# Loading the first w_in piece behind v, seven more magnitudes as VectorE masks, and other steps for the early pieces

## The chip, the cores and the metric

The kernel runs on one core of a Trainium2 chip. The metric is the device time of one execution in microseconds (us); the time given for a kernel is the median of its runs. Engines are named as in the profile: PE is TensorE, DVE is VectorE, ACT is ScalarE, POOL is GpSimd, and SP is the engine whose queue issues nearly all DMAs.

## The reference

Packed attention (32 packed queries per head, 8 batches, 8 heads, 576 tokens, 64 wide) feeds a feed-forward layer with a leaky activation:

```python
p_packed = sm_attn(p, k, v)                # 32 x 576 scores per head
out      = sm_attn(q, p_packed, p_packed)  # 576 x 32 scores per head
x = out as 4608 tokens x 512
h = x @ w_in                               # 512 x 2048
g = maximum(h, 0) + alpha * minimum(h, 0)
return g @ w_out                           # 2048 x 512
```

w_in and w_out are float64: the kernel turns them to float32 on the core, from their 32-bit words.

## The kernel before, in words

Work goes by batch b (0 to 7), each with two half-tiles of 288 tokens, k = 2b and 2b + 1. For a batch, `attention(b)` runs in small steps (it is a generator): load k, v, q; scores; softmax; `aT` (the transposed softmax) times v gives c, and its transposition p2 (p in the profile); scores against q; a second softmax over 32 entries; and the result a_f. The product h = x @ w_in is done as a @ (p2 @ w_in): `packed_w(b, j)` makes pw = p2 @ w_in for 512 columns (L375), `first(k, f)` makes 128 hidden rows (L774 in float32; L780 to L782 in split form), ACT takes the negative part (neg, L787), DVE adds the two parts to g (L801), and `second(k, f)` multiplies g by w_out into four accumulators (L896 in float32; L899 to L901 in split form). `first` writes to ps_h, a pool of two PSUM banks, so the third `first` needs the bank that the g of the one before last has set free.

w_in and w_out come in eight pieces of 1 MB each: `w_in_load`/`w_in_convert` and `w_out_load`/`w_out_convert`. A piece is converted in one of two forms. `to_f32` makes the magnitude of the upper word, then on DVE a clamp (L132), a shift (L135), the sign (L139) and the low word (L143), with ACT making the low word ready (L131). `to_half` has on DVE a clamp (L166), a shift (L169) and one addition (L177), and on ACT two instructions (L175, L176). The magnitude is one instruction in either: Abs on ACT (L151), or a mask on DVE (L123, only the first piece of w_in before).

The order is written out by hand. The string in `go` is the start: a and b are steps of attention(0) and attention(1), i and o load a piece of w_in or w_out, I and O convert one, 0 makes half of a packed product, H splits the float32 a of batch 0 in two, S splits the first pieces of w_out, n loads alpha, and u, v, w, x are spare matmuls that keep PE busy. After it come steps: step i issues `first` of the i-th (k, f) and `second` of the one two before, and `pieces` says which letters stand at which step. `PAIRS` are the steps with the packed products of both first batches. The program's scheduler then sets each engine's order; every engine works through its own order and waits at an instruction until what it needs is there. All loads go through SP's queue. An issue takes one of eight semaphores in turn and waits for the DMA that had it before.

Of the kernel before, what the change touches and what calls it, by code (L numbers as in the profile page):

```python
# [27 lines left out]
def pack_attention_ffn_kernel(  # L28
# [17 lines left out]
    nc = tc.nc  # L46
# [72 lines left out]
    def to_f32(raw, mag, on_dve=False):  # L119
        u, up, low = words(raw, "low", U32)  # L120
        bits = mag.bitcast(U32)
        if on_dve:
            nc.vector.tensor_scalar(  # L123
                out=bits, in0=u[:, :, :, 1], scalar1=0x7FFFFFFF, scalar2=None, op0=ALU.bitwise_and
            )
        else:
            magnitude(mag, up)
        with ExitStack() as behind:
            for mark in late + lows:
                behind.enter_context(tc.issue_after(mark.ins))  # L130
            lows[:] = [nc.scalar.activation(out=low, in_=u[:, :, :, 0], func=AF.Copy, scale=2.0**-29)]  # L131
        nc.vector.tensor_scalar(  # L132
            out=mag, in0=mag, scalar1=F64_BOTTOM, scalar2=F64_TOP, op0=ALU.max, op1=ALU.min
        )
        nc.vector.tensor_scalar(  # L135
            out=bits, in0=bits, scalar1=3, scalar2=0x3FFFFFF8,
            op0=ALU.logical_shift_left, op1=ALU.bitwise_and,
        )
# [8 lines left out]
    def magnitude(mag, up):  # L147
        with ExitStack() as behind:
            for ins in lows:
                behind.enter_context(tc.issue_after(ins.ins))  # L150
            nc.scalar.activation(out=mag, in_=up, func=AF.Abs)  # L151

    def to_half(raw, mag, begun=False):

        u, up, rest = words(raw, "rest", F32)
        bits = mag.bitcast(U32)
        low = rest.bitcast(U16).rearrange("p a (f t) -> p a f t", t=2)[:, :, :, 0]
        if not begun:
            magnitude(mag, up)
# [12 lines left out]
        if len(first_half) == 1:  # L178
            first_half.append(last)
# [10 lines left out]
        if written:  # L190
            queue[:] = [ins]

    first_half, begun = [], []
    last_mm, queue, written, raws, tail, whole, w0, other = [], [], [True], {}, {}, [], [], []

    def half(g):
        return g != 2

    def half_in(j):
        return j > 1  # L200

    def w_out_load(g):
        raws["o", g] = const.tile([P, 2, 512], U64, name=f"wraw{g}", tag=f"wo{g}")
# [2 lines left out]
    def w_out_convert(g):  # L206
        if g < QF:
            if not whole:
                whole.append(const.tile([P, QF, 2, 512], F32, name="wo_whole", tag="wo7"))
            mag = whole[0][:, g]  # L210
            for a in range(2):
                wo_t[2 * g + a] = mag[:, a]
        else:
            mag = cv.tile([P, 2, 512], F32, name="mag", tag="mag")
        if half(g):
            to_half(raws.pop(("o", g)), mag, g in begun)
        else:
            to_f32(raws.pop(("o", g)), mag)
        if g >= QF:
            w_out_split(g, mag)  # L220

    def w_out_begin(g):
        whole.append(const.tile([P, QF, 2, 512], F32, name="wo_whole", tag="wo7"))
        raw = raws["o", g]
        up = raw.bitcast(F32).rearrange("p a (f t) -> p a f t", t=2)[:, :, :, 1]
        nc.scalar.activation(out=whole[0][:, g], in_=up, func=AF.Abs)
        begun.append(g)
# [29 lines left out]
    def w_in_convert(n):  # L257
# [1 line left out]
        raw = raws.pop(("i", n))  # L259
        w = win.tile([P, 4, 256] if j == 0 else [P, 2, 512], F32, name="w", tag="w")  # L260
        if half_in(j):
            to_half(raw, w)
        else:
            to_f32(raw, w, n < 1)
        if j == 0:
            w0.append(w)
            for a in range(2):
# [680 lines left out]
    EARLY, XF, XJ, QF = 2, 1, 1, 2  # L948

    a0, a1 = attention(0), attention(1)  # L950
    counts = dict.fromkeys("iIoOSH01A", 0)
    BUSY = {"u": 7, "v": 4, "w": 2, "x": 3, "y": 3, "z": 2}
    BEHIND = {"v": "m0", "w": "z0", "z": "m1"}

    def go(what):


        for ch in what:
# [7 lines left out]
            elif ch in "ab":  # L966
                next(a0 if ch == "a" else a1, None)
            elif ch in counts:
                n = counts[ch]
                counts[ch] += 1  # L970
                if ch == "0":
                    if n < 2:
                        packed_w(0, 0, (n,))
                    else:
                        packed_w(0, n - 1)
                elif ch == "1":
                    packed_w(1, n, (None,) if n else (0, 1))
# [12 lines left out]
    go("inaaauoiaaaIaboaiiaa0abooavbawaOIx")  # L990
    tail.clear()
    written.clear()

# [10 lines left out]
            if b % 2 and k % 2:  # L1004
                order += [(b // 2, n, "columns") for n in range(4)]
    turns, joints, drains = {}, {}, []
    PAIRS = {13: ((1, 0), (1, 1)), 31: ((0, 2), (1, 2)), 35: ((0, 3), (1, 3))}
    for at_, pair in PAIRS.items():
        joints[at_] = [(0, packed_w_pair(*pair))]

# [7 lines left out]
                turns.setdefault(at_, []).append(gen)  # L1018
        drains.append((steps[-1], gen))

    pieces = {0: "aab", 1: "Oai0ib", 3: "bbI", 4: "I", 5: "Oob0", 6: "bbbiO", 7: "HHbb", 10: "S", 11: "S", 12: "b", 13: "bb", 14: "b", 15: "o", 17: "Io", 18: "b", 19: "I", 20: "i", 21: "o", 22: "I", 24: "I", 27: "O", 30: "O", 34: "O", 36: "O"}

    X = {1: 50, **{b: begins[b] + 8 for b in range(2, 7)}}
    Y = {1: 54, **{b: begins[b] + 22 for b in range(2, 7)}}
    for b in range(2, B):
        T, x, y = begins[b - 1], X[b - 1], Y[b - 1]
        if b == 2:
            firsts = [39, 40, 41, 42, 44, 45, 46, 47, 49]
        elif b == 3:
            firsts = [44, 50, 61, 62, 63, 64, 66, 67, 68]  # L1030
# [97 lines left out]
```

## Time and profile before

| | before |
|---|---|
| median of 3 runs | 711.91 us (711.72 to 712.71) |
| profiled execution | 712.62 us, of it span 710.8 us |
| PE busy | 695.5 us, 98% of the span |
| DVE busy | 474.3 us, 67% |
| ACT busy | 358.1 us, 50% |
| mean granted clock of PE | 0.995 of full |

The span is what the profiler saw from the first to the last instruction; the 1.8 us around it are in the time and not in the trace. PE is busy nearly all the time, so the end is set by when PE gets its work going at the start, and by each gap in it after that. The averages of DVE and ACT hide that both are full in the first stage.

### The profile page before, as it was taken

What the parts mean: (1) busy time and instruction counts of PE and PEld (TensorE: products, weight loads), DVE (VectorE), ACT (ScalarE), POOL (GpSimd) and SP (SyncE); (2) the same over time, 40 slices, a digit from 0 to 9 for tenths busy, and PEclk for the clock granted to TensorE, in tenths of its full rate; (3) what the DMA queues carried; (4) which work ended last, traced back from release to release, by engine and by line L of the source; (5) the groups of instructions that cost most, each with busy time, mean ns of one, the idle gap of its engine ahead of it and who ended that gap; (6) DMA issues with size and microseconds to landing.
All of it is one profiled execution on the core that took longest, in us unless ns stands there. A gap on an engine that the chain in (4) does not pass through costs nothing.

```text
span 710.8 us, 14597 instructions
## 1 busy us (share of the span) xinstructions
PE 695.5 (98%) x5600; PEld 599.2 (84%) x5600; DVE 474.3 (67%) x1067; ACT 358.1 (50%) x846; POOL 33.0 (5%) x128
## 2 busy tenths in 40 slices
PE   6899999999999999999999999999999999999997
PEld 3578998899898888888878888888887888798897
DVE  4999888865796568656773567846694456964443
ACT  3796788944355535444443454545353333533232
POOL 1001200001001200001000010001000000000000
PEclk9899999999999999999999999999999999999999
DMA  9996474133534422452323423334314203010100
GB/s 312 385 342 244 129 261 151 60 104 122 155 117 156 135 59 99 148 156 73 126 47 118 156 68 127 125 100 120 97 59 152 66 7 95 25 30 1 30 16 30
DMA packets 77188, 85.36 MB, mean 120 GB/s; under 512 B 34880, under 2 KB 57920, under 8 KB 77120
## 3 DMA queue, kind: packets, MB, share of 16 engines
q1 hardware_dynamic: 76480, 83.89, 36.4%
q8 instruction: 44, 0.72, 0.4%
q10 hardware_dynamic: 640, 0.56, 0.2%
q14 instruction: 24, 0.20, 0.1%
HBM read 70.79 MB, written 13.63 MB: 119 GB/s over the span
## 4 chain that ended last, share of the span: by engine, by line
PE 92%; DVE 3%; DMA 2%; ACT 2%; issue 0%; SPq 0%; DVEq 0%
PE acc L832 40%; PE ps_h L780 9%; PE ps_h L782 9%; PE ps_h L781 9%; PE acc L899 5%; PE acc L900 5%; PE acc L901 5%; PE ps_m L375 4%; PE ps_j L375 3%; PE acc L896 2%; PE acc L375 2%; DMA wraw<-in_w_out 1%; DMA xtwo<-in_kT 1%; PE ps_h L774 1%; PE spare L286 0%
## 5 line engine op out<-in xcount | busy, mean ns | idle before, releaser
L832 PE MATMUL acc<-wo,gh 128*128 128x512 f32 x704 | 200.1, 398 | 0.0
L787 ACT ACTIVATE neg<-ps_h 128x256 f32<-128x256 f32 (+2 forms) x256 | 105.4, 412 | 164.4 <-PE ps_h L782 157.8
L801 DVE SCALAR_TENSOR_TENSOR neg<-neg,nal,ps_h 128x256 f32<-128x256 f32 (+1 forms) x248 | 119.6, 483 | 77.1 <-ACT neg L787 76.6
L811 ACT CAST gh<-neg 128x256 fp32r<-128x256 f32 (+1 forms) x248 | 101.7, 411 | 111.3 <-DVE neg L801 110.0
L780 PE MATMUL ps_h<-a_h,pw 128*128 128x256 f32 (+2 forms) x496 | 146.4, 295 | 0.8 <-DVE neg L801 0.8
L782 PE MATMUL ps_h<-a_h,pw 128*128 128x256 f32 (+2 forms) x496 | 146.6, 296 | 0.0
L781 PE MATMUL ps_h<-a_l,pw 128*128 128x256 f32 (+2 forms) x496 | 146.5, 295 | 0.0
L812 DVE TENSOR_TENSOR gl<-neg,gh 128x256 fp32r<-128x256 f32 (+1 forms) x248 | 104.4, 425 | 61.5 <-ACT gh L811 59.8
L832 PEld LDWEIGHTS acc<-wo,gh 128*128 128x128 f32 x704 | 126.7, 195 | 21.9 <-issue 4.2
L832 PE MATMUL acc<-wo,gl 128*128 128x512 f32 x352 | 115.5, 394 | 0.0
L780 PEld LDWEIGHTS ps_h<-a_h,pw 128*128 128x128 f32 x496 | 93.5, 188 | 7.6 <-DVE neg L801 1.3
L781 PEld LDWEIGHTS ps_h<-a_l,pw 128*128 128x128 f32 x496 | 93.4, 188 | 7.2
L782 PEld LDWEIGHTS ps_h<-a_h,pw 128*128 128x128 f32 x496 | 93.5, 189 | 0.1
L900 PE MATMUL acc<-gh,wo 128*128 128x288 f32 (+1 forms) x280 | 79.7, 293 | 0.5 <-DVE wo L237 0.5
L832 PEld LDWEIGHTS acc<-wo,gl 128*128 128x128 f32 x352 | 68.7, 195 | 13.5
L899 PE MATMUL acc<-gh,wo 128*128 128x288 f32 (+1 forms) x280 | 80.0, 296 | 0.0
L901 PE MATMUL acc<-gl,wo 128*128 128x288 f32 (+1 forms) x280 | 69.8, 293 | 0.0
L899 PEld LDWEIGHTS acc<-gh,wo 128*128 128x128 f32 x280 | 52.6, 189 | 5.0 <-ACT pw L730 3.4
L900 PEld LDWEIGHTS acc<-gh,wo 128*128 128x128 f32 x280 | 52.8, 189 | 0.7 <-DVE wo L237 0.7
L794 DVE SCALAR_TENSOR_TENSOR rest<-neg,nal,ps_h 128x64 f32<-128x64 f32 x96 | 26.6, 277 | 40.1 <-ACT neg L787 40.1
L901 PEld LDWEIGHTS acc<-gl,wo 128*128 128x128 f32 x280 | 48.6, 188 | 0.7 <-issue 0.5
L832 PE MATMUL acc<-wo,rparts 128*128 128x512 f32 x144 | 35.3, 397 | 0.0
(157 smaller groups left out, 690.1 us busy)
## 6 DMA issues: line engine op xcount, KB each, us to landing
w<-w_whole SPq DMA_DIRECT2D x48, 512.0 KB, 5.8
wraw<-in_w_in SPq DMA_DIRECT2D x8, 1024.0 KB, 10.9
wraw<-in_w_out SPq DMA_DIRECT2D x8, 1024.0 KB, 6.8
xraw<-in_kT SPq DMA_DIRECT2D x28, 288.0 KB, 4.5
xraw<-in_qT SPq DMA_DIRECT2D x28, 288.0 KB, 4.6
vraw<-in_v SPq DMA_DIRECT2D x96, 64.0 KB, 2.1
outT<-out SPq DMA_DIRECT2D x44, 128.0 KB, 2.2
w_whole<-w SPq DMA_DIRECT2D x6, 512.0 KB, 7.6
```

The source lines that it names most:

```text
L375: mm = nc.tensor.matmul(out, lhs, rhs, start=start, stop=stop)
L780: nc.tensor.matmul(x, w[:, 0, i], a_h[:, i], start=(i == 0), stop=False)
L781: nc.tensor.matmul(x, w[:, 0, i], a_l[:, i], start=False, stop=False)
L782: mm = nc.tensor.matmul(x, w[:, 1, i], a_h[:, i], start=False, stop=(i == 1))
L787: marks[:] = [mm, nc.scalar.activation(out=neg, in_=x, func=AF.Relu, scale=-1.0)]
L801: nc.vector.scalar_tensor_tensor(out=g, in0=neg, scalar=nal[:, f : f + 1], in1=x, op0=ALU.mult, op1=ALU.add)
L811: late[:] = [nc.scalar.copy(out=gh, in_=g)]
L812: nc.vector.tensor_tensor(out=gl, in0=g, in1=fv(gh), op=ALU.subtract)
L832: mm = nc.tensor.matmul(ps, g, wo_t[f][:, part_], start=(f == 0 and i == 0), stop=(f == NF - 1 and i == 2))
L899: nc.tensor.matmul(ps, wo_t[f][:, 0, os_], gh, start=begin, stop=False)
L900: nc.tensor.matmul(ps, wo_t[f][:, 1, os_], gh, start=False, stop=False)
L901: mm = nc.tensor.matmul(ps, wo_t[f][:, 0, os_], gl, start=False, stop=end)
```

## The change

- The first piece of w_in is loaded behind v (it was ahead of it), and the second behind the k of batch 1; its loads and conversions stand at other places in the `go` string.
- The magnitude of w_in pieces 1, 3, 5, 7 and of w_out pieces 0, 1, 3, 5 is a DVE mask. The first piece of w_in, which had the only mask, has its magnitude on ACT now.
- w_in pieces 2 and 3 are converted by `to_half`, w_out pieces 3 and 4 by `to_f32`.
- Early pieces, some steps of attention(2) and attention(3), and the paired packed products stand at other steps.
- An unused helper (w_out_begin) is gone.

```diff
-    def to_half(raw, mag, begun=False):
+    def to_half(raw, mag, on_dve=False):
...
-        if not begun:
-            magnitude(mag, up)
+        magnitude(mag, u, up, on_dve)
...
+    WHOLE_OUT, HALF_IN = (2, 3, 4), (1, 2, 3)
+    ON_DVE_IN, ON_DVE_OUT = (1, 3, 5, 7), (0, 1, 3, 5)
+
     def half(g):
-        return g != 2
+        return g not in WHOLE_OUT
 
     def half_in(j):
-        return j > 1
+        return j in HALF_IN
...
-            to_f32(raw, w, n < 1)
+            to_f32(raw, w, n in ON_DVE_IN)
...
-    go("inaaauoiaaaIaboaiiaa0abooavbawaOIx")
+    go("aiaaunaaaIaobiaaboia0oiaaaavwIoObx")
...
-    PAIRS = {13: ((1, 0), (1, 1)), 31: ((0, 2), (1, 2)), 35: ((0, 3), (1, 3))}
+    PAIRS = {11: ((1, 0), (1, 1)), 32: ((0, 3), (1, 3)), 29: ((0, 2), (1, 2))}
...
-    pieces = {0: "aab", 1: "Oai0ib", 3: "bbI", 4: "I", 5: "Oob0", 6: "bbbiO", ...
+    pieces = {0: 'abbO', 1: '0a', 2: 'b', 3: 'bHabI', 4: 'bOiHI', 5: '0', 6: 'Ob', ...
```

Lines of the changed program stand five lower than those of before from `to_half`'s callers on: its L769 is L774 of before, L891 is L896, L796 is L801, L782 is L787.

**The loads on SP.** Before, from the first load on (wraw_118 and wraw_180 are the first two pieces of w_in, wraw_178 the first of w_out, xtwo the k and q of batch 0, vtwo its v, xraw the k of batch 1):

```order
L189 DMA xtwo<-in_kT 128x2x288 x3
L189 DMA wraw_118<-in_w_in 128x4x256
L189 DMA al<-in_alpha 128x16
L189 DMA vtwo<-in_v 128x2x512
L189 DMA vtwo<-in_v 64x2x128
L189 DMA vtwo<-in_v 128x2x512
L189 DMA vtwo<-in_v 64x2x128
L189 DMA xtwo<-in_qT 128x2x288 x4
L189 DMA wraw_178<-in_w_out 128x2x512
L189 DMA wraw_180<-in_w_in 128x4x256
L189 DMA praw<-in_pT 128x128
L189 DMA xraw<-in_kT 128x576 x4
```

The same place on SP in the changed program (wraw_126, wraw_234 and wraw_222 are those three pieces):

```order
L188 DMA xtwo<-in_kT 128x2x288 x3
L188 DMA vtwo<-in_v 128x2x512
L188 DMA vtwo<-in_v 64x2x128
L188 DMA vtwo<-in_v 128x2x512
L188 DMA vtwo<-in_v 64x2x128
L188 DMA wraw_126<-in_w_in 128x4x256
L188 DMA xtwo<-in_qT 128x2x288 x4
L188 DMA al<-in_alpha 128x16
L188 DMA wraw_222<-in_w_out 128x2x512
L188 DMA praw<-in_pT 128x128
L188 DMA xraw<-in_kT 128x576 x4
L188 DMA wraw_234<-in_w_in 128x4x256
```

The first piece of w_in now ends where the last of v ended, and the second where the last k of batch 1 ended.

**ACT at the start.** Before, behind the four exponentials of the first softmax (aT and c lead to p, the packed queries):

```order
L131 ACTIVATE low<-wraw_118 128x1024
L660 COPY aT<-ps_j 128x384
L660 COPY aT<-ps_j 128x256
L679 ACTIVATE c<-ps_m,den 128x64 x2
L514 COPY p_289<-ps_m 128x128
```

ACT of the changed program, at the same place:

```order
L151 ACTIVATE w<-wraw_126 128x1024
L126 ACTIVATE low<-wraw_126 128x1024
L655 COPY aT<-ps_j 128x384
L655 COPY aT<-ps_j 128x256
L674 ACTIVATE c<-ps_m,den 128x64 x2
L509 COPY p_283<-ps_m 128x128
```

Two instructions on the first piece of w_in, not one, stand ahead of the copies of aT.

**ACT up to the first neg.** Before, from the second softmax's exponential on:

```order
L551 ACTIVATE t_291<-t_291 128x576
L151 ACTIVATE wo_whole<-wraw_178 128x1024
L175 ACTIVATE rest<-wraw_178,tiny 128x1024
L176 ACTIVATE rest<-wraw_178 128x1024
L151 ACTIVATE w<-wraw_180 128x1024
L131 ACTIVATE low<-wraw_180 128x1024
L787 ACTIVATE neg<-ps_h 128x288
```

ACT of the changed program:

```order
L546 ACTIVATE t_302<-t_302 128x576
L126 ACTIVATE low<-wraw_234 128x1024
L174 ACTIVATE rest<-wraw_222,tiny 128x1024
L175 ACTIVATE rest<-wraw_222 128x1024
L782 ACTIVATE neg<-ps_h 128x288
```

Both magnitudes are gone from here, and the second piece of w_in comes first.

**DVE up to the first g.** Before, from the first half's a_f on:

```order
L568 STREAM_TRANSPOSE a_f<-t_291 128x2x288
L166 TENSOR_SCALAR wo_whole<-wo_whole 128x1024
L169 TENSOR_SCALAR wo_whole<-wo_whole 128x1024
L132 TENSOR_SCALAR w<-w 128x1024
L177 ISA wo_whole<-wo_whole,rest 128x2048
L135 TENSOR_SCALAR w<-w 128x1024
L801 SCALAR_TENSOR_TENSOR g<-neg,nal,ps_h 128x288
```

DVE of the changed program:

```order
L563 STREAM_TRANSPOSE a_f<-t_302 128x2x288
L144 TENSOR_SCALAR w<-wraw_234 128x1024
L144 TENSOR_SCALAR wo_whole<-wraw_222 128x1024
L127 TENSOR_SCALAR w<-w 128x1024
L165 TENSOR_SCALAR wo_whole<-wo_whole 128x1024
L130 TENSOR_SCALAR w<-w 128x1024
L168 TENSOR_SCALAR wo_whole<-wo_whole 128x1024
L134 SCALAR_TENSOR_TENSOR w<-wraw_234,w 128x1024
L176 ISA wo_whole<-wo_whole,rest 128x2048
L796 SCALAR_TENSOR_TENSOR g<-neg,nal,ps_h 128x288
```

Eight conversion instructions stand ahead of the first g where there were five, and the first of them needs the second piece of w_in.

**DVE and PE in the second half-tile (k = 1).** DVE of the changed program from the g of f = 0 to that of f = 1 (wraw_330 is the fourth piece of w_in, wraw_328 the third of w_out, a_l the second half's split):

```order
L796 SCALAR_TENSOR_TENSOR g<-neg,nal,ps_h 128x288
L144 TENSOR_SCALAR w<-wraw_330 128x1024
L127 TENSOR_SCALAR mag<-mag 128x1024
L165 TENSOR_SCALAR w<-w 128x1024
L130 TENSOR_SCALAR mag<-mag 128x1024
L168 TENSOR_SCALAR w<-w 128x1024
L695 TENSOR_TENSOR a_l<-a_f,a_h 128x2x288
L134 SCALAR_TENSOR_TENSOR mag<-wraw_328,mag 128x1024
L796 SCALAR_TENSOR_TENSOR g<-neg,nal,ps_h 128x288
```

PE of the changed program there, from the firsts of f = 0 and 1 (x4) to the products of f = 1:

```order
L769 MATMUL ps_h<-a_f,pw 128x288 x4
L667 MATMUL ps_m<-vraw,aT 32x64 x40
L370 MATMUL ps_m<-w,p_283 32x512 x2
L769 MATMUL ps_h<-a_f,pw 128x288 x2
L891 MATMUL acc_671<-g,wo_whole 128x288
L891 MATMUL acc_672<-g,wo_whole 128x288
L891 MATMUL acc_673<-g,wo_whole 128x288
L891 MATMUL acc_674<-g,wo_whole 128x288
L370 MATMUL ps_m<-w,p_283 32x512 x2
L769 MATMUL ps_h<-a_f,pw 128x288 x2
```

PE of before, where its uninterrupted stretch of firsts (two rows each) and products begins:

```order
L654 MATMUL ps_m<-ident,s_t 128x128 x5
L774 MATMUL ps_h<-a_f,pw 128x288 x2
L896 MATMUL acc_447<-g,wo_whole 128x288
L896 MATMUL acc_448<-g,wo_whole 128x288
L896 MATMUL acc_449<-g,wo_whole 128x288
L896 MATMUL acc_450<-g,wo_whole 128x288
L774 MATMUL ps_h<-a_f,pw 128x288 x2
```

In the changed program all sixteen products of the first half-tile are ahead of the second half-tile's firsts; before, eight of them came behind.

## Rows read from the trace of the kernel before

**Rows 1.** By stretch: us, busy (count) of PE, PEld, DVE, ACT, POOL; PEclk, DMA share, GB/s.

```profile
18.00:22.00 4.00, 1.80 (x12) 1.61 (x13) 3.86 (x8) 2.64 (x5) 0.00 (x0) 0.86 1.04 380
22.00:28.00 6.00, 6.00 (x32) 3.97 (x33) 5.03 (x8) 4.88 (x6) 0.00 (x0) 0.52 1.04 404
39.00:57.00 18.00, 18.00 (x121) 13.36 (x121) 17.96 (x28) 17.95 (x31) 0.00 (x0) 1.00 1.03 384
```

**Rows 2.** PE's waits from 60 to 700 us: total, times, longest.

```profile
PE ps_h L780 <- DVE neg L801: 0.8, 2, 0.4
...
PE ps_m L375 <- issue: 0.2, 1, 0.2
```

**Rows 3.** Loads: starts of issues (timeline, tile view), then sizes and us to landing.

```profile
2.29 0.47 SPq L189 DMA_DIRECT2D wraw<-in_w_in  x1
...
wraw<-in_w_in SPq DMA_DIRECT2D x1, 1024.0 KB, 7.3
...
L189 SPq DMA_DIRECT2D vtwo<-in_v x4: 434/630/754, 3.4 to 5.7; - x4
...
vtwo<-in_v SPq DMA_DIRECT2D x1, 64.0 KB, 8.3
...
L189 SPq DMA_DIRECT2D xraw<-in_kT x4: 328/369/501, 14.0 to 16.1; - x4
...
DMA to landing us min/median/max: 10.3/10.5/10.5
```

**Rows 4.** Timeline of ACT, 11 to 16 us: start, us.

```profile
11.14 1.17 ACT L131 ACTIVATE low<-wraw 128x1024 uint32<-128x1024 uint32 x1
12.20 0.75 ACT L660 COPY aT<-ps_j 128x384 f32<-128x384 f32 x2
...
15.74 0.27 ACT L514 COPY p<-ps_m 128x128 f32<-128x128 f32 x1 [0.42 <-PE ps_m L512]
```

**Rows 5.** Timeline of PE: aT times v, and the second scores.

```profile
13.64 1.31 PE L672 MATMUL ps_m<-vtwo,aT 128*32 128x64 f32 x76 [1.13 <-DMA vtwo<-in_v]
...
16.05 1.49 PE L375 MATMUL acc<-xtwo,p 64*32 64x288 f32 x32 [0.36 <-ACT p L514]
```

**Rows 6.** Timeline of DVE, second softmax of the first half.

```profile
17.09 0.84 DVE L525 STREAM_TRANSPOSE t<-acc 128x288 f32<-128x288 f32 x2
...
22.35 0.78 DVE L568 STREAM_TRANSPOSE a_f<-t 128x576 f32<-128x576 f32 x1
```

**Rows 7.** Timeline of ACT up to the first neg.

```profile
21.72 1.21 ACT L175 ACTIVATE rest<-wraw,tiny 128x1024 f32<-128x1024 f32 x1
22.96 1.36 ACT L176 ACTIVATE rest<-wraw 128x1024 uint16<-128x1024 uint32 x1
24.20 1.11 ACT L151 ACTIVATE w<-wraw 128x1024 f32<-128x1024 f32 x1
...
26.47 0.41 ACT L787 ACTIVATE neg<-ps_h 128x288 f32<-128x288 f32 x1
```

**Rows 8.** The chain that ended last, in order of time: start, us, what.

```profile
27.77 0.42 DVE g L801
...
37.08 0.78 DVE a_f L568
...
38.55 1.24 PE ps_h L774 x4
39.79 1.94 PE acc L896 x8
41.73 0.97 PE ps_h L774 x4
...
45.61 0.55 PE ps_m L654 x5
```

**Rows 9.** Groups of DVE instructions, 12.4 to 60 us: count, busy, mean ns, idle before.

```profile
L139 DVE SCALAR_TENSOR_TENSOR w<-wraw,w 128x1024 uint32<-128x1024 uint32 x4 | 4.9, 1221 | 0.1
L132 DVE TENSOR_SCALAR w<-w 128x1024 f32<-128x1024 f32 x4 | 2.8, 691 | 0.9 <-ACT w L151 0.9
```

More of the change, by code (lines that the diff above doesn't have):

```diff
@@ L121, in to_f32 @@
         bits = mag.bitcast(U32)
[L122 to L126, printed above, removed]
-            magnitude(mag, up)
+        magnitude(mag, u, up, on_dve)
         with ExitStack() as behind:
@@ L145, in to_f32, with magnitude @@
             first_half.append(last)
-    def magnitude(mag, up):
+    def magnitude(mag, u, up, on_dve):
+        if on_dve:
+            nc.vector.tensor_scalar(
+                out=mag.bitcast(U32), in0=u[:, :, :, 1], scalar1=0x7FFFFFFF, scalar2=None, op0=ALU.bitwise_and
+            )
+            return
         with ExitStack() as behind:
@@ L163, in to_half @@
         low = rest.bitcast(U16).rearrange("p a (f t) -> p a f t", t=2)[:, :, :, 0]
-        if not begun:
-            magnitude(mag, up)
+        magnitude(mag, u, up, on_dve)
         nc.vector.tensor_scalar(
@@ L191, in load @@
             queue[:] = [ins]
-    first_half, begun = [], []
+    first_half = []
     last_mm, queue, written, raws, tail, whole, w0, other = [], [], [True], {}, {}, [], [], []
+    WHOLE_OUT, HALF_IN = (2, 3, 4), (1, 2, 3)
+    ON_DVE_IN, ON_DVE_OUT = (1, 3, 5, 7), (0, 1, 3, 5)
     def half(g):
-        return g != 2
+        return g not in WHOLE_OUT
     def half_in(j):
-        return j > 1
+        return j in HALF_IN
     def w_out_load(g):
@@ L215, in w_out_convert @@
         if half(g):
-            to_half(raws.pop(("o", g)), mag, g in begun)
+            to_half(raws.pop(("o", g)), mag, g in ON_DVE_OUT)
         else:
-            to_f32(raws.pop(("o", g)), mag)
+            to_f32(raws.pop(("o", g)), mag, g in ON_DVE_OUT)
         if g >= QF:
             w_out_split(g, mag)
[L222 to L227, printed above, removed]
     def w_out_late_split(g):
@@ L261, in w_in_convert @@
         if half_in(j):
-            to_half(raw, w)
+            to_half(raw, w, n in ON_DVE_IN)
         else:
-            to_f32(raw, w, n < 1)
+            to_f32(raw, w, n in ON_DVE_IN)
         if j == 0:
@@ L950, in pack_attention_ffn_kernel @@
     a0, a1 = attention(0), attention(1)
-    counts = dict.fromkeys("iIoOSH01A", 0)
+    counts = dict.fromkeys("iIoOSH01", 0)
     BUSY = {"u": 7, "v": 4, "w": 2, "x": 3, "y": 3, "z": 2}
@@ L979, in go @@
                     with ExitStack() as behind:
-                        for ins in tail.values() if ch != "A" else []:
+                        for ins in tail.values():
                             behind.enter_context(tc.issue_after(ins.ins))
@@ L983, in go @@
                             "i": w_in_load, "I": w_in_convert, "o": w_out_load,
-                            "O": w_out_convert, "S": w_out_late_split, "H": late_a, "A": w_out_begin,
+                            "O": w_out_convert, "S": w_out_late_split, "H": late_a,
                         }[ch](n)
@@ L1019, in add @@
         drains.append((steps[-1], gen))
-    pieces = {0: "aab", 1: "Oai0ib", 3: "bbI", 4: "I", 5: "Oob0", 6: "bbbiO", 7: "HHbb", 10: "S", 11: "S", 12: "b", 13: "bb", 14: "b", 15: "o", 17: "Io", 18: "b", 19: "I", 20: "i", 21: "o", 22: "I", 24: "I", 27: "O", 30: "O", 34: "O", 36: "O"}
+    pieces = {0: 'abbO', 1: '0a', 2: 'b', 3: 'bHabI', 4: 'bOiHI', 5: '0', 6: 'Ob', 7: 'b', 10: 'Si', 11: 'bSobb', 12: 'o', 13: 'b', 14: 'iIb', 15: 'i', 16: 'b', 19: 'b', 20: 'I', 22: 'o', 24: 'I', 25: 'I', 27: 'o', 28: 'O', 31: 'O', 33: 'O', 36: 'O'}
     X = {1: 50, **{b: begins[b] + 8 for b in range(2, 7)}}
-    Y = {1: 54, **{b: begins[b] + 22 for b in range(2, 7)}}
+    Y = {1: 56, **{b: begins[b] + 22 for b in range(2, 7)}}
     for b in range(2, B):
@@ L1027, in pack_attention_ffn_kernel @@
         if b == 2:
-            firsts = [39, 40, 41, 42, 44, 45, 46, 47, 49]
+            firsts = [37, 41, 42, 42, 43, 44, 44, 47, 48]
         elif b == 3:
-            firsts = [44, 50, 61, 62, 63, 64, 66, 67, 68]
+            firsts = [47, 50, 61, 61, 63, 64, 65, 68, 74]
         else:
```

## Prediction

> **What bounds the kernel now.** I read the stretches first. From 39 to 57 us PE is busy the whole time, and so are DVE and ACT [rows 1]. From 60 to 700 us three kinds of wait keep PE idle, the first 0.8 us and the last 0.2 us in total, 1.5 us together [rows 2]. So PE's list of work sets the end, and a change can move the end only by moving the time at which PE begins to work without a break, by the work that is then still left, or by opening a gap later. The chain that ended last says when that is: at 38.55 us a first of the half-tile k = 0 starts, and from there the chain is PE alone for many rows [rows 8]. Ahead of it the chain is DVE: the first g (27.77 us) and the second half's a_f (37.08 us, done 37.85) [rows 8]. Further ahead lies the softmax of batch 0: PE multiplies aT by v and had to wait 1.13 us for v [rows 5], ACT writes p at 15.74 us [rows 4], the scores follow at 16.05 us [rows 5], DVE takes them at 17.09 us and finishes the first a_f at 23.1 us [rows 6].
>
> **The loads: when the two pieces land now.** DMAs of SP's queue land in the order of issue. The first piece of w_in was issued at 2.29 us and landed 7.3 us later, at 9.6 us; the last part of v was issued at 5.7 us and landed 8.3 us later, at 14.0 us [rows 3]. The two trade places and the bytes ahead are the same, so v should land near 11.3 us (14.0 less the 2.7 us or so by which a megabyte delays it at the 380 to 404 GB/s of these stretches [rows 1]) and the piece near 14.0 us. The bound below is 13.0 us, if it lags its bytes no more than it did at 9.6 us. In the same way the second piece of w_in now lands where the last k of batch 1 did: issued at 16.1 us and 10.5 us to landing, 26.6 us [rows 3]. I take 26.5 us, with 25.5 us as the early bound.
>
> **Part one, ACT ahead of aT: 2.0 us later.** Loading v first takes away the 1.13 us wait [rows 5]. But on ACT the magnitude and the low word of the first piece stand ahead of the two copies of aT, as the low word alone did, which then had no wait since its data had landed at 9.6 us: it ran at 11.14 us and the copies at 12.20 us [rows 4]. Now ACT stands at the magnitude until 14.0 us. Then come 1.12 us (the other magnitude, 1.11 us [rows 7]), 1.17 us and the copies' 0.75 us [rows 4], about 16.9 us with their overlap. Only then can PE do its second half of aT times v, half of the 1.31 us [rows 5], that is 0.66 us. From the end of that product (14.95 us) to p it was 0.8 us [rows 4, 5]. So p starts at 18.35 us instead of 15.74, 2.6 us later. DVE had taken the scores 0.3 us late, being busy with the conversion, and that slack is used up: the second softmax begins 2.3 us later, the first a_f is done at 25.4 us. With a landing at 13.0 us it is 1.3 us. I take 2.0 us: a_f at 25.1 us.
>
> **Part two, ACT and DVE ahead of the first g: 1 us more when PE is full.** On ACT the low word of w_in's second piece now stands ahead of the two rests of w_out's first piece and of the first neg. It waits for 26.5 us, and 1.17 us, 1.21 us and 1.36 us [rows 4, 7] less overlap bring neg to 30.0 us, where it was 26.47 us [rows 7]. On DVE eight conversions are ahead of g from 26.5 us on: six of 0.69 us and two of 1.22 us [rows 9], 6.6 us, a little less back to back, so g is at 33.0 us against 27.77 us [rows 8]. The magnitudes taken from ACT (1.11 us each) thus help little: ACT waits for data, and DVE, which was full, has them at 0.69 us each [rows 7, 9]. Before, DVE took 9.7 us from that g's end to the end of the second half's a_f (28.19 to 37.85 us [rows 8]), without a pause to speak of. In the changed order a mask and a clamp (0.65 us each), two more g (0.42 us each [rows 8]), a reduction and a split (0.75 us each, like the other passes over 576 columns [rows 6]) have come in between and one sign (1.14 us) has gone ahead of g: 12.2 us. The a_f is then done at 45.6 us, and PE runs without a break from 45.9 us. That looks like 7.4 us, but most of it is work done earlier: when PE of before began at 38.55 us it had 24 products of the float32 part ahead of it, and the changed one has 16, since all products of k = 0 now precede the firsts of k = 1. Eight products are twice 1.94 us [rows 8]; with one set of transposes (0.55 us [rows 8]) it is 4.4 us. PE of before was at the same point at 38.55 + 4.4 = 42.95 us. The loss is 45.9 - 42.95 = 2.9 us, in which the 2.0 us of part one are contained. With the early landings of both pieces it is 1.5 us.
>
> **Part three, a bank that comes free late: 2.0 us.** In the second half-tile PE's first of f = 3 stands ahead of the four products of f = 1 and needs the ps_h bank that the g of f = 1 frees. On DVE that g now stands seven instructions behind the g of f = 0: mask, two clamps, two shifts (0.69 us, about 0.6 back to back), a split of 0.7 us and a sign of 1.22 us [rows 9], 5.3 us with g's own 0.42 us [rows 8]. Between the two events PE has the first of f = 2 (0.97 us [rows 8]), four products (1.94 us [rows 8]) and a quarter of a packed product, 3.2 us. PE waits the other 2.1 us, and I take 2.0 us. Bounds: nothing, if DVE has run ahead through its list, and 2.1 us. PE is full here otherwise, so a gap is a loss in full.
>
> **The rest.** The two pieces of w_in that go to the half form save one DVE instruction of 1.22 us each, the two pieces of w_out that leave it cost as much again, and the masks of the later pieces stand at stretches where PE waits 1.5 us in all [rows 2]. The moved pieces and packed products past 60 us can win at most that and could open gaps of the same kind, 0.4 to 0.5 us each; I take nothing, from -0.5 to +0.5 us. Loading alpha later costs nothing: POOL needs it before the first g only.
>
> **The sum.** 2.9 + 2.0 = 4.9 us, rounded to 5.0 us. On the profiled execution that makes 712.62 + 5.0 = 717.6 us. That execution is 0.7 us above the median of the runs shown, so the time is forecast at 711.91 + 5.0 = **716.9 us**.
>
> **A rule against the row.** The trace shows the first 3.4 MB (k, v and the piece) landing by 14.0 us [rows 3]. The Trainium skill's page "DMA: Bandwidth & Descriptors" (section "Specifications") gives the fabric a ceiling of 435 GB/s, and its section "Anatomy of one DMA" a fixed cost of about 2 us. By these the piece would land near 1.25 + 8.0 + 2.0 = 11.2 us, an estimate from that page, just as ACT gets to it. The trace speaks against it, and the first rival below says what it would bring.
>
> **Rivals.** (1) Faster: both pieces land before ACT gets to them, the first by 11.2 us and the second by 22.5 us. Then part one turns into a gain of 0.2 us (the wait for v goes, the magnitude and the low word on ACT take most of it back). DVE goes from the first a_f at 22.9 us through eight conversions to g at 29.3 us and, without waits for ACT, to the second a_f at 41.2 us. PE is full from 41.3 us against 42.95 us, a gain of 1.7 us. DVE is ahead then and the bank's wait shrinks to 0.8 us. Net -0.9 us, 711.0 us. For it speaks that all the added DVE work fits; against it that the landing times above come from the same bytes in the same queue. It decides below a landing of about 12 us for the first piece and 23.5 us for the second. (2) Slower still, by PE's clock: from 18 to 22 us PE was busy 1.80 of 4 us, and its granted clock in the next stretch was 0.52 of full, that is near 1.2 GHz, until 28 us [rows 1]. In the changed order PE has little to do from 29 to 33 us, as it waits for ACT's copies and for g. If the clock falls there too, the products and packed products from 33 us on take twice as long for some 4 us, half of it on the way to the next g: 2.1 us more, 719.0 us. (3) The milder case: the pieces land at the early bounds and DVE catches up, so that the bank's wait doesn't appear: 1.5 to 2 us, 713.9 us. (4) The change moves the time by nothing that shows, where the earlier v and the later pieces cancel: 711.9 us.
>
> **How the numbers follow.** The forecast has a chance of 0.40, rival 2 0.18, rival 3 0.17, rival 4 0.08, rival 1 0.17. The likeliest case's own range is 715.0 to 718.3 us. The range that should hold the time 8 times in 10 leaves out rival 1 and the upper end of rival 2: 711.5 to 720.3 us. Faster or slower by over 0.2% (1.4 us), about what a measurement of this kernel can tell from no change: slower 0.75 (the forecast, rivals 2 and 3), same 0.14 (rival 4 and the part of rival 1 whose 0.9 us lies within it), faster 0.11 (the rest of rival 1, where its gain is larger or later gaps go too).
>
> **What would show it right or wrong.** Right: the timeline of ACT has its magnitude of the first piece start at 13 to 14 us with an idle time before it that a DMA ended, p starts near 18 us, ACT's next wait for a DMA ends near 26.5 us, the first g is near 33 us, the chain turns into PE alone near 46 us, and PE waits some 2 us for a g of the second half-tile near 54 us. Wrong: no such wait on ACT; an a_f before 23 us; or a chain that is PE alone before 43 us. If the firsts start as forecast and the end doesn't move, gaps past 57 us have closed that I count as nothing.

## The result, and the profile after

| | before | changed |
|---|---|---|
| median | 712.04 us (711.72 to 712.71, 4 runs) | 719.63 us (717.77 to 721.29, 4 runs) |
| profiled execution | 712.62 us, span 710.8 | 717.77 us, span 716.0 |
| PE busy | 695.5 us | 700.1 us |
| DVE busy | 474.3 us | 479.6 us |
| ACT busy | 358.1 us | 351.6 us |

The changed kernel is slower: 1.0105 times the time of before (95% interval 1.0075 to 1.0135). The forecast was 716.9 us, in a range of 711.5 to 720.3 us. The profiled execution took 5.15 us longer than that of before, where the sum of the prediction had 5.0 us; the median is 7.6 us longer. So two things are to be explained: the 5.15 us, and why the median lies 1.9 us above the execution that was profiled.

ACT first, its timeline (start, us, line, operation, and in brackets the idle time before it and what ended it). It answers [rows 4, 7]:

```profile
13.37 1.12 ACT L151 ACTIVATE w<-wraw 128x1024 f32<-128x1024 f32 x1 [2.37 <-DMA wraw<-in_w_in]
...
15.42 0.74 ACT L655 COPY aT<-ps_j 128x384 f32<-128x384 f32 x2
...
17.68 0.27 ACT L509 COPY p<-ps_m 128x128 f32<-128x128 f32 x1 [0.57 <-PE ps_m L507]
...
25.99 1.18 ACT L126 ACTIVATE low<-wraw 128x1024 uint32<-128x1024 uint32 x1 [3.56 <-DMA wraw<-in_w_in]
...
29.63 0.38 ACT L782 ACTIVATE neg<-ps_h 128x288 f32<-128x288 f32 x1
```

Twice ACT stands still until a piece of w_in lands, and each time work of the attention or of the first hidden rows is behind it. DVE, answering [rows 6] and the DVE part of [rows 8]:

```profile
24.56 0.78 DVE L563 STREAM_TRANSPOSE a_f<-t 128x576 f32<-128x576 f32 x1
25.99 0.69 DVE L144 TENSOR_SCALAR w<-wraw 128x1024 uint32<-128x1024 uint32 x1 [0.65 <-DMA wraw<-in_w_in]
...
31.89 0.51 DVE L796 SCALAR_TENSOR_TENSOR g<-neg,nal,ps_h 128x288 f32<-128x288 f32 x1
...
43.37 0.77 DVE L563 STREAM_TRANSPOSE a_f<-t 128x576 f32<-128x576 f32 x1
```

PE, answering [rows 5] and the PE part of [rows 8]:

```profile
15.94 0.77 PE L667 MATMUL ps_m<-vtwo,aT 128*32 128x64 f32 x40 [3.22 <-ACT aT L655]
...
18.00 2.18 PE L370 MATMUL acc<-xtwo,p 64*32 64x288 f32 x32 [0.35 <-ACT p L509]
...
30.36 0.99 PE L370 MATMUL ps_m<-xraw,praw 64*32 64x288 f32 x16 [0.63 <-ACT s_t L593]
32.45 2.21 PE L891 MATMUL acc<-g,wo_whole 128*128 128x288 f32 x8 [1.10 <-DVE g L796]
...
44.81 2.11 PE L769 MATMUL ps_h<-a_f,pw 128*128 128x288 f32 x8
...
48.39 1.05 PE L370 MATMUL ps_m<-w,p 64*32 64x512 f32 x4
...
52.48 1.05 PE L370 MATMUL ps_m<-w,p 64*32 64x512 f32 x4
53.64 1.24 PE L769 MATMUL ps_h<-a_f,pw 128*128 128x288 f32 x4
...
56.75 1.06 PE L370 MATMUL ps_m<-w,p 64*32 64x512 f32 x8
...
61.51 0.51 PE L775 MATMUL ps_h<-a_h,pw 128*128 128x288 f32 x1
```

PE of before, with the same work:

```profile
50.94 1.09 PE L375 MATMUL ps_m<-w,p 64*32 64x512 f32 x16
...
55.73 0.51 PE L780 MATMUL ps_h<-a_h,pw 128*128 128x288 f32 x1
...
56.56 1.50 PE L672 MATMUL ps_m<-vraw,aT 128*32 128x64 f32 x80
57.99 0.40 PE L782 MATMUL ps_h<-a_h,pw 128*128 128x288 f32 x1
```

The firsts of k = 1 start at 44.81 us in the changed kernel; by the prediction's own count of the products left, before was there at 42.95 us. PE then shows no wait worth naming up to 61.51 us, yet it has lost another 2.5 us by then: before began its split part at 55.73 us, and as it still had aT times v of batch 1 to do (1.43 us to the next row), it was at the same point at 57.16 us. The loss at 61.51 us is thus 4.35 us. The rows show where PE put it: the packed product of 16 matmuls (counted as in the trace, which has two for each float32 matmul of the program), one row of 1.09 us before, comes in portions of 4, 4 and 8, and each takes about as long as the whole did. The chain that ended last says who asked for that time; from 42.55 to 53.64 us it is on ACT and DVE alone, and on DVE from one g to the next:

```profile
47.39 0.51 DVE g L796
47.91 0.60 DVE w L144
48.51 0.66 DVE mag L127
49.17 0.80 DVE w L165
49.97 0.17 DVE mag L130
...
50.69 0.67 DVE w L168
51.36 0.25 DVE a_l L695
...
51.95 1.21 DVE mag L134
53.16 0.44 DVE g L796
...
53.64 1.24 PE ps_h L769 x4
```

From 60 to 700 us PE waits 1.0 us in two kinds of wait, where it was 1.5 us [rows 2]; with the second scores of batch 1, half of which come in two portions as well (0.69 us each, where one row took 0.72 us before), the end comes out 5.15 us late. By stretch, the five columns of busy time being PE, PEld, DVE, ACT and POOL, and the first number behind them the granted clock of PE, against [rows 1]:

```profile
18.00:22.00 4.00, 4.00 (x52) 2.13 (x53) 3.21 (x6) 0.89 (x3) 0.00 (x0) 0.50 1.06 390
22.00:28.00 6.00, 5.70 (x31) 4.82 (x38) 5.21 (x11) 2.44 (x3) 0.00 (x0) 0.58 1.14 312
28.00:33.00 5.00, 3.27 (x38) 1.50 (x27) 5.00 (x7) 3.19 (x7) 0.00 (x0) 1.00 0.97 328
33.00:39.00 6.00, 5.98 (x38) 4.09 (x37) 6.00 (x11) 4.90 (x10) 0.00 (x0) 1.00 1.01 370
39.00:57.00 18.00, 17.56 (x152) 11.86 (x154) 16.68 (x31) 16.60 (x29) 1.64 (x2) 1.00 1.00 378
```

From 39 to 57 us neither DVE nor ACT is full any more. The masks and forms took 6.5 us of work off ACT in all; before 33 us it stood waiting for loads instead, 2.37 us, 3.56 us and, ahead of 32.70 us, 1.78 us.

### The profile page after: what moved, and what is told of

The parts are those of the page before. It is cut to its first block, busy times and chain, and to the rows that moved or that the text cites. A ratio compares the mean times of both kernels' runs of the same rounds, so it can differ in the third digit from the quotient of the medians.

```text
span 716.0 us, 14595 instructions
## 1 busy us (share of the span) xinstructions
PE 700.1 (98%) x5600; PEld 600.1 (84%) x5600; DVE 479.6 (67%) x1074; ACT 351.6 (49%) x839; POOL 34.7 (5%) x128
## 4 chain that ended last, share of the span: by engine, by line
PE 84%; DVE 8%; DMA 3%; ACT 2%; issue 1%; SPq 0%; DVEq 0%; ACTq 0%
PE acc L827 39%; PE ps_h L775 9%; PE ps_h L777 9%; PE ps_h L776 9%; PE acc L894 4%; PE acc L895 4%; PE acc L896 4%; PE ps_m L370 3%; PE ps_j L370 2%; DVE pw L726 1%; DMA wraw<-in_w_in 1%; PE acc L370 1%; PE acc L891 1%; DMA xtwo<-in_qT 1%; DMA vtwo<-in_v 1%
## 5 line engine op out<-in xcount | busy, mean ns | idle before, releaser
L782 ACT ACTIVATE neg<-ps_h 128x256 f32<-128x256 f32 (+2 forms) x256 | 104.8, 410 | 167.1 <-PE ps_h L777 156.7
L796 DVE SCALAR_TENSOR_TENSOR neg<-neg,nal,ps_h 128x256 f32<-128x256 f32 (+1 forms) x248 | 119.5, 483 | 80.4 <-ACT neg L782 79.9
L807 DVE TENSOR_TENSOR gl<-neg,gh 128x256 fp32r<-128x256 f32 (+1 forms) x248 | 107.5, 437 | 58.6 <-ACT gh L806 56.4
L894 PE MATMUL acc<-gh,wo 128*128 128x288 f32 (+1 forms) x280 | 79.4, 296 | 0.1
L895 PE MATMUL acc<-gh,wo 128*128 128x288 f32 (+1 forms) x280 | 78.5, 293 | 0.0
L896 PE MATMUL acc<-gl,wo 128*128 128x288 f32 (+1 forms) x280 | 67.9, 294 | 0.0
L896 PEld LDWEIGHTS acc<-gl,wo 128*128 128x128 f32 x280 | 47.7, 188 | 0.8 <-issue 0.5
```

What stands on the lines that cost most here:

```text
L782: marks[:] = [mm, nc.scalar.activation(out=neg, in_=x, func=AF.Relu, scale=-1.0)]
L796: nc.vector.scalar_tensor_tensor(out=g, in0=neg, scalar=nal[:, f : f + 1], in1=x, op0=ALU.mult, op1=ALU.add)
L807: nc.vector.tensor_tensor(out=gl, in0=g, in1=fv(gh), op=ALU.subtract)
L894: nc.tensor.matmul(ps, wo_t[f][:, 0, os_], gh, start=begin, stop=False)
L895: nc.tensor.matmul(ps, wo_t[f][:, 1, os_], gh, start=False, stop=False)
L896: mm = nc.tensor.matmul(ps, wo_t[f][:, 0, os_], gl, start=False, stop=end)
```

## Experiments

Each was compared with the kernel before, run beside it (712.28 us, 712.47 us, 712.54 us and 712.55 us in the four groups of runs).

**The same kernel again.** No edit.

> The changed kernel once more, to see what spreads its executions. Theory (waits for landings): ACT's magnitude of the first piece starts between 13.2 and 14.0 us, its low word of the second between 25.5 and 26.6 us, and the first g is at 31.5 to 33 us; an execution that takes 2 or 3 us longer has later landings or a PE at half clock for longer than until 28 us. Rival (DVE's added work alone): the start is the same in all executions and the spread comes from past 64 us. Both: 717.5 to 721.5 us.

720.33 us (718.65 to 721.79, 5 runs), 1.0108 (1.0092 to 1.0124). Its profiled execution took 721.79 us, 4.0 us longer than the other one, so the two traces tell what executions of one program differ in. PE and, below, the clock by stretch:

```profile
31.23 0.99 PE L370 MATMUL ps_m<-xraw,praw 64*32 64x288 f32 x16 [2.08 <-ACT s_t L593]
33.34 4.21 PE L891 MATMUL acc<-g,wo_whole 128*128 128x288 f32 x8 [1.11 <-DVE g L796]
...
38.51 2.62 PE L891 MATMUL acc<-g,wo_whole 128*128 128x288 f32 x8
...
48.34 2.11 PE L769 MATMUL ps_h<-a_f,pw 128*128 128x288 f32 x8
```

```profile
22.00:28.00 6.00, 4.81 (x43) 3.50 (x42) 4.96 (x10) 2.19 (x5) 0.00 (x0) 0.97 1.08 308
28.00:33.00 5.00, 2.14 (x20) 0.89 (x20) 5.00 (x8) 3.76 (x7) 0.00 (x0) 0.96 0.80 249
33.00:39.00 6.00, 5.67 (x25) 3.24 (x26) 5.76 (x10) 3.45 (x6) 0.00 (x0) 0.50 1.00 364
```

The eight products of the first g took 4.21 us where they took 2.21 us: from 33 us PE ran at 0.50 of full clock, 1.2 GHz. From the first product to the firsts of k = 1 it is 15.00 us here (33.34 to 48.34) and 12.36 us there (32.45 to 44.81): the clock costs 2.64 us. The rest of the 4.0 us is a start 0.89 us later and half a microsecond behind it. What came before differs in two things. Here the loads landed later: ACT got to the first piece at 14.26 us and to the second at 26.88 us (13.37 and 25.99 us there), both a little past what was expected, so its copies of the scores came 0.9 us later too. And PE was back at full clock from 22 us (0.97 in the first row), so its own work was done 0.6 us earlier. Together it stood idle 2.08 and 1.11 us (2.14 us busy of 5 here, 3.27 us there); in the other execution PE was near half clock up to 28 us (0.58), still had work at 29.7 us and idled 0.63 and 1.10 us. This is rival 2 of the prediction, in one of the two traced executions of this kernel.

**The gap filled.** In the changed kernel, eight matmuls of the identity, which nothing reads, directly behind the firsts of f = 1.

```diff
+    def keep_warm(n):
+        spare = ps_a.tile([P, 512], F32, name="spare", tag="acc3")
+        with tc.issue_after(last_pe[0].ins):
+            for _ in range(n):
+                nc.tensor.matmul(spare[:, :P], ident, ident, start=True, stop=True)
...
         if i == AHEAD - 1:
+            keep_warm(8)
```

> The changed kernel with eight matmuls of the identity with itself between the firsts of f = 1 and the second scores of batch 1 (some 2.1 us of PE, in the gap near 29 to 31 us); nothing reads their product. Theory (PE's idle time there lets its clock fall to half from 33 us on in most executions, the products that take 2.2 us then take 4.2): the granted clock from 33 to 39 us is 1.00, the products of the first g take 2.2 us, the median falls by 2 us or so to 717.5 to 718.5 us. Rival (the clock falls for another reason, or is no part of the time): 720 us, or 0.5 us more as the scores come later; the products at 4.2 us as before in the longer executions.

719.19 us (718.87 to 720.01, 5 runs), 1.0093 (1.0079 to 1.0106). PE's timeline:

```profile
28.48 1.95 PE L275 MATMUL spare<-ident 128*128 128x128 f32 x16
...
32.67 2.21 PE L897 MATMUL acc<-g,wo_whole 128*128 128x288 f32 x8 [1.08 <-DVE g L802]
35.84 0.94 PE L376 MATMUL ps_m<-w,p 64*32 64x256 f32 x16 [0.96 <-ACT s_t L599]
```

PE was at full clock by 24 us, about as early as in the longer execution, but it idled only 1.08 us ahead of the products; the clock stayed up from 33 to 39 us (1.00) and they took 2.21 us. So in this stretch the clock fell behind PE's idle time, and with that filled it did not. Of the 2 us or so that theory expected in the median, 0.4 to 1.1 us came. The scheduler, seeing eight more matmuls, put ACT's copy of the scores behind one more conversion, which costs PE the 0.96 us in the last row and 0.70 and 0.76 us further on. So the mechanism is seen in one trace, and its share of the median isn't measured by this run. What speaks for a share is the spread: the five runs here lie within 1.14 us, the nine of the changed kernel within 4.02 us. Nor is idle time all that decides: from 18 to 22 us PE was busy 1.80 us of 4 before [rows 1], 1.79 us with the forms alone and 1.85 us with one mask (both below), and its clock from 22 to 28 us was 0.52, 1.00 and 1.00.

**The second packed product in one row.** In the changed kernel, the 16 matmuls are issued as one chain, with the heads in reverse order.

```diff
-            for pr, r, rs, cs in heads():
+            for pr, r, rs, cs in reversed(list(heads())) if (b, j) == (0, 1) else heads():
...
+                        chained.append(True)
                         packed_w(0, n - 1)
+                        chained.clear()
```

> The changed kernel with one edit: the second packed product of batch 0 stands in one row on PE (16 matmuls, and so the scores behind it), instead of in portions of 4, 4 and 8 between the products of k = 1. Theory (a portion of 4 takes as long as 16, about 1.05 us, since matmuls of different quadrants overlap): PE's busy time falls by 2 us and the end comes 1.5 to 2.5 us earlier than the changed kernel's, 718.0 us if that is at 719.9. Rival (PE had slack there, so the split is free): no change. Rival (the product stands in the way of the firsts, which then come late): 0.5 to 1 us slower.

719.84 us (717.98 to 720.82, 5 runs), 1.0099 (1.0084 to 1.0113): no change against the changed kernel, as the first rival had it. But the portions are not free, as that rival assumed; the trace tells why nothing is won:

```profile
56.60 1.24 PE L769 MATMUL ps_h<-a_f,pw 128*128 128x288 f32 x4 [2.20 <-DVE g L796]
...
61.65 1.09 PE L370 MATMUL ps_m<-w,p 64*32 64x512 f32 x16
```

Without the portions PE waits 2.20 us for DVE's g at the first of f = 3. The two costs lie on top of each other: as long as that g is late, a packed product cut in pieces only fills PE's wait.

**The first load alone.** The kernel before, with one edit.

```diff
-    go("inaaauoiaaaIaboaiiaa0abooavbawaOIx")
+    go("ainaauoiaaaIaboaiiaa0abooavbawaOIx")
```

> The kernel before with one edit: the load of w_in's first piece goes to SP's queue behind v instead of ahead of it. Nothing else moves on any engine. Theory of the prediction (a later landing costs through the aT copies on ACT): the low word on ACT starts at 13.4 to 14.0 us instead of 11.14, the aT copies near 14.5 us instead of 12.20, p at 16.6 to 17.2 us instead of 15.74, the end 0.7 to 1.8 us later, about 713.2 us. Rival (v earlier takes away PE's wait of 1.13 us and DVE has room for the later piece): 0.3 to 0.8 us faster than before. Rival (the landing doesn't matter): within 0.3 us of before.

713.44 us (712.85 to 714.34, 11 runs), 1.0013 (1.0004 to 1.0022), 0.97 us by the medians. As theory had it: ACT's low word starts at 13.59 us, p at 16.75 us.

```profile
13.59 1.15 ACT L131 ACTIVATE low<-wraw 128x1024 uint32<-128x1024 uint32 x1 [2.35 <-DMA wraw<-in_w_in]
...
16.75 0.27 ACT L514 COPY p<-ps_m 128x128 f32<-128x128 f32 x1 [0.42 <-PE ps_m L512]
```

**Forms and masks alone, order alone.** First the masks and forms of the changed kernel with all of before's orders (the `go` string, PAIRS, pieces, firsts, Y); then the changed kernel with before's masks and forms:

```diff
-    WHOLE_OUT, HALF_IN = (2, 3, 4), (1, 2, 3)
-    ON_DVE_IN, ON_DVE_OUT = (1, 3, 5, 7), (0, 1, 3, 5)
+    WHOLE_OUT, HALF_IN = (2,), (2, 3)
+    ON_DVE_IN, ON_DVE_OUT = (0,), ()
```

> The masks and the four pieces' other form alone, all in the order of the kernel before (its loads, steps, pairs and firsts). Theory (the moved steps and the load are what costs, the masks bring little): 712 to 713.5 us, a little above before, since DVE is full from 25 to 38 us and takes three masks of 0.69 us more there while ACT, which is relieved, waits for data. Rival (the masks and forms are what costs): 715 to 719 us. Rival (they bring time, as ACT is full too from 39 to 57 us): 710.5 to 711.5 us.

> The other half: loads, steps, pairs and firsts of the changed kernel, with the masks on ACT and the forms as in the kernel before. Theory (the order is what costs): 718 to 722 us, like the changed kernel, and up to 1.5 us more as ACT has magnitudes of 1.1 us ahead of the first neg. Rival (the masks and forms cost): 712 to 714 us.

Forms and masks in the old order: 715.18 us (714.13 to 716.28, 5 runs), 1.0037 (1.0024 to 1.0049). The new order with old forms and masks: 724.77 us (723.85 to 725.15, 4 runs), 1.0171 (1.0157 to 1.0184). The first is at the lower end of the rival and above the theory, the second above even the theory's upper end of 723.5 us. Order costs 12.3 us by itself, forms and masks 2.7 us by themselves, and all together 7.6 to 8.0 us: the masks and forms win back 4.3 to 4.7 us of what the order costs. ACT of the order alone, and PE:

```profile
27.34 1.13 ACT L151 ACTIVATE w<-wraw 128x1024 f32<-128x1024 f32 x1 [5.50 <-DMA wraw<-in_w_in]
```

```profile
33.48 1.49 PE L370 MATMUL ps_m<-xraw,praw 64*32 64x288 f32 x16 [5.56 <-ACT s_t L593]
...
37.84 5.15 PE L891 MATMUL acc<-g,wo_whole 128*128 128x288 f32 x16
```

ACT stands 5.50 us at the second piece of w_in; then two magnitudes more than in the changed kernel are ahead of its copies of the scores, for which PE waits 5.56 us, and the clock falls (0.51 from 33 to 39 us).

**Masks alone, forms alone, one mask alone,** each in the order of before. One mask is `n < 2` in place of `n < 1` for w_in.

> The masks as the changed kernel has them (w_in's pieces 1, 3, 5, 7 and w_out's 0, 1, 3, 5; w_in's piece 0 back on ACT), in the order and with the forms of the kernel before. The masks and forms together, in that order, took 715.18 us against 712.47. Theory (DVE is the full engine from 23 to 57 us, each mask of 0.6 us there is paid by the end where ACT was not what DVE waited for): 713.5 to 715 us, most of the 2.7 us. Rival (the forms are what costs, one mask alone moved nothing): 712 to 713 us.

> The four pieces in the other form alone (w_in's 2 and 3 to the half form, w_out's 3 and 4 out of it), masks and order as in the kernel before. Theory (the half form saves one DVE instruction of 1.2 us for each of the two w_in pieces ahead of 57 us, the other two pieces pay it back later under PE): 711.5 to 713 us. Rival (the forms cost, through ACT's rests of 1.2 and 1.4 us ahead of the second aT): 713.5 to 715 us.

> The kernel before with one of the seven masks alone: w_in's second piece gets its magnitude from DVE instead of ACT; PE's order is the same. Theory (a mask pays where DVE stood waiting for ACT's magnitude): DVE's wait of 0.90 us for that magnitude goes, the mask takes 0.6 us of DVE, ACT is 1.1 us earlier at the first neg, so the end comes 0.2 to 0.5 us earlier, 711.7 us. Rival (DVE is full from 23 to 38 us and every mask is a loss there): 0.3 to 0.6 us slower.

Masks: 713.72 us (12 runs), 1.0013 (1.0004 to 1.0021), at the lower edge of the theory. Forms: 715.52 us (5 runs), 1.0044 (1.0032 to 1.0057); the theory fell, and the rival holds, with 0.5 us more than it had. Masks and forms cost 1.2 and 3.0 us apart and 2.7 us together, so the two don't add up. The half form saves DVE an instruction but costs ACT two rests of 1.25 and 1.36 us per piece where the low word took 1.17 us, and ACT was full there [rows 1]. So neg comes late (46.22 us) and PE waits for g:

```profile
47.26 1.24 PE L769 MATMUL ps_h<-a_f,pw 128*128 128x288 f32 x4 [1.41 <-DVE g L796]
```

One mask: 712.51 us (11 runs), 0.9995 (0.9986 to 1.0003). DVE's wait for the magnitude of 0.90 us [rows 9] is gone, but the time doesn't show it: neither theory nor rival came true. None of the kernels beat the one before.

**Loads and steps at the start, in the changed kernel.** Three strings for `go`; in order: the second piece loaded ahead of batch 1's k; the first piece converted three steps later; both pieces loaded where before had them.

```diff
-    go("aiaaunaaaIaobiaaboia0oiaaaavwIoObx")
+    go("aiaaunaaaIaoibaaboia0oiaaaavwIoObx")
...
+    go("aiaaunaaaaobiaaIboia0oiaaaavwIoObx")
...
+    go("iaaaunaaaIaoibaaboia0oiaaaavwIoObx")
```

> The second piece of w_in is loaded ahead of the k of batch 1 again; no engine's order but SP's changes. Theory (waits for landings): it lands near 23.4 us, but the first half's a_f comes at 25.3 us in the changed kernel because of the first piece, and DVE does the conversions behind it, so g comes at 31.2 instead of 31.9 us and the time falls by 0.7 us only. Rival (the second landing alone is the cause): ACT and DVE start 2.6 us earlier and the time falls by 2 to 2.6 us. Rival (DVE's added work): no change.

> The loads stay as in the changed kernel; the first piece is converted three steps later, so that on ACT its two instructions stand behind the copies of aT, behind c and behind p. Theory (waits for landings): p starts at 14.4 us instead of 17.7, but ACT still stands until 26 us for the second piece ahead of the first neg, so the first g stays within 1 us of 31.9 and the time falls by 0 to 1 us. Rival (the wait ahead of aT is the cause by itself): the time falls by 2 to 2.6 us. Two scores of batch 1 that PE had in two portions stand in one row here, worth 0.3 to 0.7 us by either.

> All else as in the changed kernel, the first two pieces of w_in loaded where they were before (ahead of v, and behind the first piece of w_out). Theory (waits for landings): the first piece lands at 9.6 us and ACT waits for neither, p starts near 15.7 us, the first a_f is done near 23.1 us, the first g is at 29.3 us, and the time falls by 2.5 to 3.3 us, to about 715.0 us on an execution like that of 717.8. Rival (DVE's added work and the order of the conversions): the first g stays past 31 us and the time falls by less than 1 us.

The second piece early: 718.17 us (718.0 to 719.93, 4 runs), 2.2 us below the changed kernel run beside it, which is what the rival had and not the theory's 0.7 us; the intervals overlap, though (1.0072 to 1.0106 against 1.0092 to 1.0124). ACT waits only 0.24 us there and neg is at 26.55 us instead of 29.63, but g is only 1.0 us earlier, at 30.93 us, since DVE has eight conversions ahead of it, as the theory said. Where the rest of the 2.2 us comes from isn't shown. Converting later: 721.51 us (4 runs), 1.2 us more where up to 1 us less was expected. p is at 15.22 us, 2.5 us earlier, and then the packed product waits 2.37 us for the converted piece and the second softmax of DVE has the conversion in its midst, so the firsts are at 29.55 us instead of 26.51. Loads back: 720.97 us (4 runs), where 2.5 to 3.3 us less than the changed kernel were expected. The first neg is at 27.11 us, 2.5 us earlier, and the first g at 30.18 us, where 29.3 was expected; p is at 17.11 us and not near 15.7, in an execution whose first exponentials ended 1.8 us later than in the first trace, and ACT still waits 2.05 us for the second piece. But the second piece of w_out is issued at 28.35 us (26.97 and 27.95 us in the two traces of the changed kernel), and ACT has its conversion, as there, ahead of a copy of the scores:

```profile
34.29 1.25 ACT L174 ACTIVATE rest<-wraw,tiny 128x1024 f32<-128x1024 f32 x1 [4.93 <-DMA wraw<-in_w_out]
```

```profile
35.87 1.37 PE L370 MATMUL ps_m<-w,p 64*32 64x256 f32 x16 [2.93 <-ACT s_t L593]
37.17 4.21 PE L891 MATMUL acc<-g,wo_whole 128*128 128x288 f32 x8
```

PE idles 2.93 us, the clock falls, the products take 4.21 us. The wait that was taken away at one load came back at the next, with the clock on top of it. So the loss does not hang on those two landings alone: with both loads back, the rest of the new order costs as much, 8.7 us against the kernel before.

## Why the prediction was right, and where it wasn't

**Part one, the landing ahead of aT.** Forecast: ACT's magnitude at 14.0 us, p at 18.35 us, a_f done at 25.1 us. Measured: 13.37 us, 17.68 us, 25.34 us (24.56 and 0.78), 2.2 us later than before instead of 2.0. That this agrees is in part luck: p was late by 1.94 us and not 2.6, but the scores behind it took 2.18 us, in a stretch granted 0.50 of full clock, where they took 1.49 us before [rows 5], and the prediction had no such term. The load alone, with the magnitude left on DVE, moves p by 1.01 us and the end by 0.97 us. The estimate of 11.2 us from the page "DMA: Bandwidth & Descriptors" of the Trainium skill (sections "Specifications" and "Anatomy of one DMA") doesn't agree with the waits that the DMA ended at 13.37 and 13.59 us; the measurement decides, and rival 1, which needed it, did not happen. That section of the Trainium skill's page gives the fixed cost for DMAs of the gpsimd path, and these loads go through SP.

**Part two, the second piece ahead of the first g.** ACT's wait ended at 25.99 us (forecast 26.5), neg was at 29.63 (30.0), g at 31.89 (33.0), the second a_f done at 44.14 (45.6). DVE went through the eight conversions in 5.9 us, not 6.6. PE was at the firsts of k = 1 at 44.81 us, not 45.9: a loss of 1.86 us where the forecast had 2.9. This term was 1.0 us too large.

**Part three, the bank.** Forecast: seven instructions between the g of f = 0 and that of f = 1, 2.0 us of waiting. The chain lists the seven, 5.8 us from one g to the next (forecast 5.3). In the trace of the changed kernel there is no such wait on PE, and the portions of 1.05 us, where the prediction counted a quarter of the product, take its place; the chain turns into PE alone at 53.64 us, at the end of this stretch, not near 46 us. With the product in one row the wait is there, 2.20 us. So the size and the cause hold, and what the prediction missed is that a portion of 4 of these matmuls takes as long as 16: 1.05 us against 1.09. The page "TensorEngine Tiling (Array Packing)" of the Trainium skill (section "Key Properties") says that tiles of the array work independently and can run in parallel; the row of 16 agrees with it, since its 16 matmuls take 0.60 us each and 1.09 us together. Three portions in place of one row are 2.1 of the 2.5 us lost from 44.81 to 61.51 us, of which 2.0 were forecast.

**The sum.** 1.86 and 2.5 us make 4.35 us at 61.51 us against 4.9, and 0.8 us come after that (the split scores among them, forecast 0 ± 0.5): 5.15 us against 5.0. A term 1.0 us too large and two that were 0.5 and 0.8 us too small cancel. So it is luck that the sum comes within 0.2 us; its terms come within 1.0 us.

**The median.** It lies within the range, but above the likeliest case's own 715.0 to 718.3 us and nearest to rival 2's 719.0 us. The step that failed is the one that took the sum of one execution for the median's. Rival 2 was priced at 2.1 us and given 0.18. In the second profiled execution of the same kernel it happened and cost 2.64 us; by the granted clock from 33 to 39 us it also happened where the packed product is in one row (0.53) and with the order alone (0.51), in part with the second piece early (0.73) and with the loads back (0.68), and not in the first execution, with the gap filled or with the later conversion (1.00). The prediction let it depend on how little PE has to do from 29 to 33 us, and took that for the same in every execution. But PE's clock from 22 to 28 us differs from execution to execution: where the packed product is in one row, ACT's copies came as in the first execution (PE went on at 30.37 and 30.36 us), PE had full clock early, idled 1.72 us there instead of 0.63, and was slow afterwards. In how many of the untraced executions it happened isn't known: the mean granted clock does not tell them apart (0.995 stands beside 718.54 us and 721.29 us), since half clock early and half clock late look the same in a mean.

**What the change didn't bring.** Masks and forms together win 4.3 to 4.7 us in the changed order, where ACT, held up by loads, has no time to make the magnitudes; which of the two wins it was not run apart. In the old order the masks cost 1.2 us and the forms 3.0 us. For the forms the trace points to ACT; for the masks the reason isn't shown.

## What to carry to other kernels

An engine that works in order turns a late load into a late everything behind it, so before a load is moved back, look at what stands behind its first consumer on that engine, and at the next load too: removing one such wait (loads back) brought it back at the next. Look also at the clock of the stretch behind a gap: in the longer execution PE idled 3.2 us, and the half clock after it took 2.64 us more. Time that a slow engine leaves to another may be filled with inefficient work which then looks like the cause; making that work efficient moved nothing here, as the slow engine was no earlier.

## What the runs showed of the hardware that was not expected

The half clock from 22 to 28 us (0.58) cost nothing in the first execution: its first products began at 32.45 us, and at 32.50 us where the packed product is in one row and the clock was full there (1.00), since they wait for DVE's g. Full clock early was worth nothing there and came before a fall: of the traces in the new order with the gap unfilled, the five with 0.93 or more from 22 to 28 us all had 0.50 to 0.73 from 33 to 39 us, and the two with 0.50 and 0.58 had 1.00. The one that can be compared lost 2.64 us by it. Matmuls of 64 rows and 32 columns take 1.05 us in portions of 4, 1.06 us in one of 8, and 1.09 us in one of 16, where little else changed; scores of 288 columns likewise, 0.72 us for 16 and 0.69 us for each half.
